# Normalised tokens of twelve tiles turned by VectorE and through DRAM, instead of by TensorE, between two attention loops

## The chip, the cores and the metric

The kernel runs on one core of a Trainium2 chip. The engines that matter here are TensorE (PE in the profile, with its weight loads as PEld), VectorE (DVE), ScalarE (ACT), GpSimd (POOL) and SyncE (SP), which issues nearly all transfers. Each engine works its instructions off in the order in which the built program has them; where one needs another's result it waits at that place, and all that stands behind it on its engine waits with it. The metric is the device time of one execution, in microseconds.

## The reference

Four layers with residuals act on x, 2048 tokens by 576 features: A, B, A, B. A is multi-query attention with 32 query heads of 18 and one shared key and value head; B is a linear attention with a learned feature map. Both begin with a layer norm without weights:

```python
def _layernorm(x, axis=-1, eps=1e-5):
    m = jnp.mean(x, axis=axis, keepdims=True)
    v = jnp.var(x, axis=axis, keepdims=True)
    return (x - m) / jnp.sqrt(v + eps)
...
def _A_ref(x, wq, wk, wv, wo):
    q = (x @ wq).reshape(B, S, H, Dh).transpose(0, 2, 1, 3)
    k = x @ wk
    v = x @ wv
    p = softmax(einsum("bhqd,bkd->bhqk", q, k) * (Dh ** -0.5))
    o = einsum("bhqk,bkd->bhqd", p, v)
    return o.transpose(0, 2, 1, 3).reshape(B, S, H * Dh) @ wo
...
x = x + _A_ref(_layernorm(x), A_wq, A_wk, A_wv, A_wo)
x = x + _B_ref(_layernorm(x), B_wqkv, B_w_phi, B_wo)
x = x + _A_ref(_layernorm(x), A_wq, A_wk, A_wv, A_wo)
x = x + _B_ref(_layernorm(x), B_wqkv, B_w_phi, B_wo)
```

The case concerns the step from the first B to the second A: the layer norm of the second A, and the products with `wq`, `wk` and `wv` that follow it.

## The kernel before

The tokens are cut into 16 tiles of 128. A pair of layers A, B is worked as one **loop** (`attend`), which computes scores, exponentials and sums of attention and, among them, the keys and features of the B layer that follows. There are two such loops, up to about 1217 us and from about 1450 us on. The stretch **between the loops** finishes the first B and prepares the second A, and only it is changed. (Behind the second loop the same read-out runs without the preparation.)

Between the loops each token tile is a job, `token_tile(i)`, a Python generator that gives up its turn at each `yield STAGE`:

- It loads the tile's features from DRAM (`load_features`, L698 and L699, `pht`) and its residual (`xt`).
- `read_out` multiplies features by the state (L804), divides by the denominators (L811 to L813) and copies the last 64 columns a second time (L814). The result `xo` is turned by five TensorE transposes into PSUM (`transposed`, L307 four at once, L311 the last), and split into an upper and a lower half, `xs`, by ScalarE (L132, L313) and VectorE (L135, L316). The output projection follows (L257, 28 matmuls), and VectorE adds it to the residual (L321).
- `next_queries`: `ln_stats` on VectorE (L283 to L286), POOL's power for the reciprocal root (L288), the bias `lnb` on VectorE (L290); `layer_norm` on ScalarE writes `xn` (L297) and copies its last 64 columns a second time (L298). `xn` is in the pool `bw`, with one buffer. Five TensorE transposes turn it, and the two halves go to `xsc`, 9 slots by 256 tokens, which two tiles share.
- After every second tile `project_queries` is queued: 5 blocks of 14 matmuls (L452), whose results ScalarE copies out (L474) and VectorE splits and squares (L478, L479), transfers to the query store `qd` (L481) and to the keys (L486), then values and norms (L492 to L503), stored to `mxd` (L504). The text calls the block of tiles 2p and 2p+1 query block p.

The rows of one block are the 14 products of an upper or lower slot with an upper or lower weight; the third of them is the first that reads a lower slot of the tokens:

```python
PRODUCTS = [p for k in range(4) for p in ((k, 0, k), (k, 1, k), (5 + k, 0, k))]
PRODUCTS += [(4, 0, 4), (4, 1, 4)]
```

`pipelined` starts one job a round and lets each active job do one stage a round, then the queued late work (query blocks). So a round with a query block is long and the next one is short; a pair of them handles two tiles. A scheduling pass then orders the instructions of each engine by dependencies, buffers and estimated durations. Between the loops nothing else fixes that order, except TensorE's in `leave`, at its beginning.

The second way of turning a tile, used inside the loops, exists already: `block_transpose` turns 32x32 blocks on VectorE (L702) and writes the blocks to their places in the DRAM tile `flipped` with four transfers (L707); `fetch_tokens` reads them back with the features on the partitions, in three transfers (L720, L722).

After the last query block `first_queries` loads the queries and shifts of the first chunk of the second loop, `q0` (in the room of `wclo`) and `q1` (in that of `xs`), by L558 and L565.

Of the kernel before, what the change touches and what calls it, by code (L numbers as in the profile page):

```python
# [9 lines left out]
F32 = mybir.dt.float32  # L10
# [3 lines left out]
AF = mybir.ActivationFunctionType  # L14
# [5 lines left out]
P = 128  # L20
S = 2048
D = 576
H = 32
DH = 18
NT = S // P
KT = 5
# [26 lines left out]
STAGE = None  # L53
# [9 lines left out]
def kernel(ctx, tc, x_in, wq, wk, wv, wo, wqkv, w_phi, wob, out):  # L63
    nc = tc.nc
    V, A, T, G = nc.vector, nc.scalar, nc.tensor, nc.gpsimd
# [6 lines left out]
    bw = ctx.enter_context(tc.tile_pool(name="bw", bufs=1))  # L72
# [57 lines left out]
    def split(dst_hi, dst_lo, src, hi_engine, lo_engine):  # L130
        if hi_engine is A:
            A.activation(dst_hi, src, AF.Copy)  # L132
        else:
            hi_engine.tensor_copy(dst_hi, src)
        lo_engine.tensor_sub(dst_lo, src, dst_hi.bitcast(F32))  # L135
# [137 lines left out]
    def run(gen):  # L273
        for _ in gen:
            pass

    def ln_stats(tiles):
        n = len(tiles)
        mv = small.tile([P, n, 2], F32, name=f"mv{n}", bufs=5)
        for j, i in enumerate(tiles):  # L280
            bn = small.tile([P, 2, 6], F32, name="bnst")
            for s in range(2):
                V.bn_stats(bn[:, s, :], xres[i][:, s * HALF : (s + 1) * HALF])  # L283
            V.bn_aggr(mv[:, j, :], bn)
        var = small.tile([P, n], F32, name=f"var{n}", bufs=5)
        V.tensor_scalar(var, mv[:, :, 1], EPS, None, op0=ALU.add)  # L286
        rstd = small.tile([P, n], F32, name=f"rstd{n}", bufs=5)
        G.tensor_tensor(rstd, var, neghalf[:, :n], op=ALU.pow)  # L288
        bias = small.tile([P, n], F32, name=f"lnb{n}", bufs=5)
        V.scalar_tensor_tensor(bias, mv[:, :, 0], -1.0, rstd, op0=ALU.mult, op1=ALU.mult)  # L290
        return {i: (rstd[:, j : j + 1], bias[:, j : j + 1]) for j, i in enumerate(tiles)}

    def layer_norm(i, stats, pool, E, tag="xn"):
        rstd, bias = stats[i]
        xn = pool.tile([P, 5 * P], F32, name=tag)
        if E is A:
            A.activation(xn[:, :D], xres[i], AF.Identity, scale=rstd, bias=bias)  # L297
            A.activation(xn[:, D:], xn[:, 512:D], AF.Copy)  # L298
        else:
            V.tensor_scalar(xn[:, :D], xres[i], rstd, bias, op0=ALU.mult, op1=ALU.add)  # L300
            V.tensor_copy(xn[:, D:], xn[:, 512:D])
        return xn

    def transposed(xn, xs, ps, hi_engine, lo_engine=V):
        pa = ps.tile([P, 4, P], F32, name="ps")
        for k in range(4):
            T.transpose(pa[:, k, :], xn[:, k * P : (k + 1) * P], idf)  # L307
        split(xs[:, 0:4, :], xs[:, 5:9, :], pa, hi_engine, lo_engine)
        yield -440
        pb = ps.tile([P, P], F32, name="ps")  # L310
        T.transpose(pb, xn[:, 512:], idf)  # L311
        if hi_engine is A:
            A.activation(xs[:, 4, :], pb, AF.Copy)  # L313
        else:
            V.tensor_copy(xs[:, 4, :], pb)
        lo_engine.tensor_sub(xs[64:P, 4, :], pb[64:P, :], xs[64:P, 4, :].bitcast(F32))  # L316
        yield -110
# [6 lines left out]
    flipped = dram.tile([NT, D, P], F32, name="flipped")  # L324
# [115 lines left out]
    def project_queries(p, layer, w, xsc, bw, pool, ps, norms):  # L440
# [15 lines left out]
        if opening:  # L456
# [3 lines left out]
            for n in range(len(PRODUCTS)):  # L460
                if n == TURN:
                    st["turn"]()
# [238 lines left out]
    def block_transpose(blocks, src, dst, pause=0):  # L701
        V.transpose(blocks, src)  # L702
        for _ in range(pause):
            yield
        for q in range(P // 32):
            rows = slice(q * 32, (q + 1) * 32)
            nc.sync.dma_start(dst[:, rows].rearrange("(b f) t -> f b t", f=32),  # L707
                              blocks[rows, :].rearrange("f (b t) -> f b t", t=32))
            yield
# [4 lines left out]
        blocks = bw.tile([P, NKG, P], F32, name="pht").rearrange("p a b -> p (a b)")  # L714
        run(block_transpose(blocks[:, :D], xres[i], flipped[i]))

    def fetch_tokens(i):
        xt = bw.tile([P, KT * P], F32, name="xn").rearrange("p (a b) -> p a b", b=P)
        src = flipped[i]
        nc.sync.dma_start(xt[:, 0:4, :], src[:512].rearrange("(k p) t -> p k t", p=P))  # L720
        for half in range(2):
            nc.sync.dma_start(xt[half * 64 : half * 64 + 64, 4, :], src[512:])  # L722
        return xt
# [98 lines left out]

    def next_queries(i, stats, layer, st, xpool, sp, ps):
        p, tt = divmod(i, PAIR)
        xn = layer_norm(i, stats or ln_stats([i]), xpool, A)
        yield STAGE
        if tt == 0:
            st["xsc"] = sp.tile([P, 9, PW], F32R, name="xsc")
        xsc = st["xsc"]
        yield from transposed(xn, xsc[:, :, tt * P : (tt + 1) * P], ps, A)  # L830
        yield STAGE
        if tt == PAIR - 1:
            st["late"].append(project_queries(p, layer, st["wq"], xsc, bw, sp, ps, st["norms"]))
# [34 lines left out]
            load_shifts(q, layer, 0, g)  # L868

    PREP = 1  # L870
    TURN = 11
    WE = V
    LOE = V
# [330 lines left out]
    with first, tc.tile_pool(name="ps0", bufs=7, space=PSUM) as ps:  # L1204
        sp = s0
        stats = {}

        def first_tile(i):
            if i % PAIR == 0:
                stats.update(ln_stats(range(i, i + PAIR)))  # L1210
            yield from next_queries(i, stats, 0, st, sp, sp, ps)
# [12 lines left out]
        ps = Banks([(ps, "ps")])  # L1224
# [54 lines left out]
    for layer in range(LAYERS):  # L1279
        last = layer == LAYERS - 1  # L1280
        st.update(start_state(bw), added=set(), loaded=set())
        with tc.tile_pool(name="a1o", bufs=2) as a1o:
# [12 lines left out]
            def stream(v, layer=layer):  # L1295
# [71 lines left out]
                def flip(i, stats):  # L1367
                    nonlocal fetched
                    unflipped.remove(i)
                    spoiled.add(i)  # L1370
                    flip_tokens(i, stats)
                    fetched = i, fetch_tokens(i)
# [68 lines left out]
            ps = psx.enter_context(tc.tile_pool(name=f"ps{layer}", bufs=7, space=PSUM))  # L1441
            ps = Banks([(ps, "ps")])
# [6 lines left out]
            with tc.tile_pool(name=f"tail{layer}", bufs=1) as tail:  # L1449
                on = st["heads_in"]()  # L1450
                load_part(on.bitcast(F32), c, 0)
                xn = layer_norm(c - 1, ln_stats([c - 1]), bw, A)
                kept = st["kept"]
                first_keys = keys_in(KEPT, kept, feature_room("featk"), st, ps)
                closing = last_group(st["last"], on, c, ps, tail)
                advance(first_keys)
                next(closing)
                advance(first_keys)
                run(closing)
                advance(first_keys)  # L1460
                xs = bw.tile([P, 9, P], F32R, name="xs2")
                advance(transposed(xn, xs, ps, A, LOE), 2)
                advance(first_keys)
                second_keys = keys_in(c - 1, xs, feature_room("featx"), st, ps)
                advance(second_keys, 2)
                advance(first_keys)
                for b in range(2):
                    po = ps.tile([P, HALF], F32, name="ps")
                    run(project(po, st["wo"], b * HALF, on))
                    add_residual(c, b, po)  # L1470
                stats = ln_stats([c])
                advance(second_keys, 2)

        with psx, tc.tile_pool(name=f"s{layer + 1}", bufs=2) as sp:
            if not last:
                reload_w4(sp)

            def leave():
                xn = layer_norm(c, stats, sp, A, "xo")
                advance(second_keys)  # L1480
                xl = sp.tile([P, 9, P], F32R, name="xs3")
# [42 lines left out]
            def token_tile(i):  # L1524
                pht = room(i)
                load_features(pht, spills[layer], i)
                if i not in left:
                    xres[i] = sp.tile([P, D], F32, name="xt", bufs=6)
                    nc.sync.dma_start(xres[i], xd[i])
                yield STAGE  # L1530
                yield STAGE
                yield from read_out(i, pht, st, sp, ps)
                if last:
                    nc.sync.dma_start(out[i * P : (i + 1) * P, :], xres[i])
                else:
                    nc.sync.dma_start(xd[i], xres[i])
                    yield STAGE
                    yield from next_queries(i, None, layer + 1, st, bw, sp, ps)
# [38 lines left out]
```

## Time and profile before

| | |
|---|---|
| Time, median of 3 | 2676.86 us (2673.14 to 2677.76) |
| Profiled execution | 2676.42 us, span 2674.6 us |
| Mean granted TensorE clock | 0.991 |
| The token tiles between the loops | about 1270 to 1447 us of the span |
| First score of the second loop | 1448.62 us |

All rows come from one execution. A row of the engines' events has the start in us, the duration, the engine (SPq is SyncE's issuing of transfers, its duration that of the issue and not of the transfer), the line, the operation, output<-inputs, shapes and the count; in square brackets the idle time ahead of it and who ended it. The first number of a window's row is its start and end.

### The profile page before, as it was taken

Reading aid. Unit: us, or ns where it says so; the run is one execution under the profiler, and the core shown is the slowest. Engines: PE = TensorE matmul, PEld = TensorE weight load, DVE = VectorE, ACT = ScalarE, POOL = GpSimd, SP = SyncE. Lnnn points to the kernel's source line nnn. Section 1 sums busy time; section 2 is a strip of 40 time slices with the busy share of each in tenths; the row PEclk is TensorE's granted clock in tenths of the full one; section 3 lists DMA queues with packets and bytes.
Section 4 is the critical chain, followed back from the end, with each engine's and each line's share of the span. In section 5 each row is a group of like instructions: output and inputs, shape, how many; then the busy total and the mean of one; then the engine's idle time right before and its main releaser. Section 6 shows DMA issues by size and latency. Waiting matters only on the chain. (4 is left out here: it accounts for less than half of the span.)

```text
span 2674.6 us, 55524 instructions
## 1 busy us (share of the span) xinstructions
PE 2602.2 (97%) x22002; PEld 1442.2 (54%) x22002; DVE 1265.0 (47%) x2871; ACT 2153.8 (81%) x2529; POOL 66.0 (2%) x106
## 2 busy tenths in 40 slices
PE   7989999999999999999999999999999999999999
PEld 6633454445444444438996344444444444444498
DVE  8435354444444444436774424444444444444265
ACT  4588889989999999994334999999999999999821
POOL 1000000000000000002000000000000000000010
PEclk9999999999999999999999999999999999999999
DMA  5466243222222222225643312222222222222164
GB/s 182 144 146 171 70 127 100 59 53 60 60 59 57 55 57 57 59 66 158 188 152 105 105 51 59 60 60 60 59 60 59 60 60 57 56 55 55 48 196 140
DMA packets 491634, 232.97 MB, mean 87 GB/s; under 512 B 237734, under 2 KB 458214, under 8 KB 491366
## 3 DMA queue, kind: packets, MB, share of 16 engines
q1 hardware_dynamic: 489894, 226.37, 31.4%
q8 instruction: 177, 2.90, 0.5%
q10 hardware_dynamic: 1472, 2.95, 0.4%
q14 instruction: 91, 0.75, 0.1%
HBM read 130.62 MB, written 96.67 MB: 85 GB/s over the span
## 5 line engine op out<-in xcount | busy, mean ns | idle before, releaser
L1047 ACT ACTIVATE pt<-sc 128x1024 f32<-128x1024 f32 x2036 | 1923.4, 1054 | 180.4 <-PE sc L574 160.3
L574 PE MATMUL sc<-qst,kst 56*128 56x512 f32 x3840 | 698.6, 452 | 21.0 <-ACT pt L1047 20.6
L574 PEld LDWEIGHTS sc<-qst,kst 56*128 56x128 f32 x3840 | 319.4, 185 | 561.7 <-ACT pt L1047 511.8
L853 PE MATMUL acc<-pt,vst 128*32 128x512 f32 x4096 | 499.8, 600 | 0.1
L853 PE MATMUL ps<-pt,vst 128*32 128x512 f32 x4048 | 486.7, 604 | 6.1 <-DVE featq L607 3.2
L853 PEld LDWEIGHTS ps<-pt,vst 128*32 128x32 f32 x4048 | 109.8, 110 | 234.0 <-issue 226.1
L853 PEld LDWEIGHTS acc<-pt,vst 128*32 128x32 f32 x4096 | 104.6, 109 | 211.7 <-issue 209.2
L321 DVE TENSOR_TENSOR xc<-xc,acc 128x288 f32<-128x288 f32 x60 | 27.3, 455 | 349.5 <-PE acc L257 349.5
L257 PE MATMUL ps<-wahi,xs 128*128 128x288 f32 x702 | 152.5, 304 | 2.5 <-ACT xs L132 1.9
L257 PE MATMUL ps<-wchi,xs 128*128 128x288 f32 x576 | 127.2, 307 | 0.0
L257 PE MATMUL acc<-wdhi,on 128*128 128x288 f32 x540 | 120.6, 309 | 3.3 <-DMA on<-od 3.3
L257 PEld LDWEIGHTS ps<-wahi,xs 128*128 128x128 f32 x702 | 116.1, 190 | 7.1 <-ACT xs L132 2.6
L257 PE MATMUL ps<-walo,xs 128*128 128x288 f32 x390 | 114.9, 297 | 0.0
L452 PE MATMUL ps<-xsc,wbhi 128*128 128x256 f32 x576 | 107.3, 285 | 0.6 <-ACT xsc L132 0.6
L474 ACT ACTIVATE pc<-ps 128x256 fp32r<-128x256 f32 x80 | 30.4, 384 | 94.0 <-PE ps L452 92.5
L257 PEld LDWEIGHTS ps<-wchi,xs 128*128 128x128 f32 x576 | 94.1, 188 | 19.0 <-issue 18.1
L607 DVE COPY featk<-acc 128x288 f32<-128x288 f32 x50 | 22.8, 457 | 172.0 <-PE acc L257 172.0
L132 ACT ACTIVATE xs<-ps 128x512 fp32r<-128x512 f32 x36 | 21.4, 595 | 102.6 <-PE ps L307 102.6
L257 PEld LDWEIGHTS acc<-wdhi,on 128*128 128x128 f32 x540 | 88.8, 189 | 25.0 <-issue 23.6
L257 PE MATMUL acc<-wahi,xs 128*128 128x288 f32 x450 | 100.0, 308 | 0.5
L257 PE MATMUL ps<-wclo,xs 128*128 128x288 f32 x320 | 94.3, 295 | 0.0
L452 PEld LDWEIGHTS ps<-xsc,wbhi 128*128 128x128 f32 x576 | 91.2, 192 | 1.6 <-ACT xsc L132 1.1
(261 smaller groups left out, 3062.3 us busy)
## 6 DMA issues: line engine op xcount, KB each, us to landing
qst<-qd SPq DMA_DIRECT2D x360, 72.0 KB
od<-parts SPq DMA_DIRECT2D x512, 36.0 KB
pht<-phi SPq DMA_DIRECT2D x32, 540.0 KB
qd<-pc SPq DMA_DIRECT2D x64, 256.0 KB
on<-od SPq DMA_DIRECT2D x60, 256.0 KB
phi<-pht SPq DMA_DIRECT2D x104, 144.0 KB
xd<-xc SPq DMA_DIRECT2D x33, 288.0 KB
flipped<-pht SPq DMA_DIRECT2D x112, 72.0 KB
```

The costliest lines, as they stand in the source:

```text
L132: A.activation(dst_hi, src, AF.Copy)
L257: T.matmul(dst, xs[:, slot, :], w[half][:, k, c0 : c0 + HALF], start=(n == 0), stop=(n == last))
L321: V.tensor_add(xr, xr, po)
L452: T.matmul(po, lhs, xsc[:, slot, :], start=(n == 0), stop=(n == LASTP))
L474: A.activation(pc[:, 0, :], po, AF.Copy)
L574: T.matmul(sc, kst[head_rows(h), t * P : (t + 1) * P], q[head_rows(h), h // 2, :], start=True, stop=True)
L607: V.tensor_copy(e[:, hs, 0, :], src)
L853: T.matmul(acc[32 * j : 32 * j + 32, :], vst[:, t, :], pts[j], start=first, stop=last)
L1047: A.activation(pt, sc, AF.Exp, scale=SCALE)
```

## The change

For layer 1, that is between the loops, and for tiles 0 to 11 (`NEAR` is 12), `next_queries` turns `xn` in the second way. ScalarE leaves out the second copy of 64 columns. VectorE turns 32x32 blocks of `xn` into `xb`; four transfers write them to `flipped[i]`; `fetch_tokens` reads them into `xf`, three transfers. `xb` and `xf` are new tiles with one buffer each. One stage later ScalarE and VectorE split `xf` into `xsc`; the sources are in SBUF and no longer in PSUM. Tiles 12 to 15 are handled as before. So sixty TensorE transposes go, and 12 VectorE transposes and 84 transfers come; a tile has one stage more.

```diff
-    def layer_norm(i, stats, pool, E, tag="xn"):
+    def layer_norm(i, stats, pool, E, tag="xn", twice=True):
...
             A.activation(xn[:, :D], xres[i], AF.Identity, scale=rstd, bias=bias)
-            A.activation(xn[:, D:], xn[:, 512:D], AF.Copy)
+            if twice:
+                A.activation(xn[:, D:], xn[:, 512:D], AF.Copy)
...
-    def fetch_tokens(i):
-        xt = bw.tile([P, KT * P], F32, name="xn").rearrange("p (a b) -> p a b", b=P)
+    def fetch_tokens(i, pool=bw, tag="xn", **kw):
+        xt = pool.tile([P, KT * P], F32, name=tag, **kw).rearrange("p (a b) -> p a b", b=P)
...
     def next_queries(i, stats, layer, st, xpool, sp, ps):
         p, tt = divmod(i, PAIR)
-        xn = layer_norm(i, stats or ln_stats([i]), xpool, A)
+        far = layer > 0 and i < NEAR
+        xn = layer_norm(i, stats or ln_stats([i]), xpool, A, twice=not far)
         yield STAGE
+        if far:
+            blocks = sp.tile([P, D], F32, name="xb", bufs=1)
+            run(block_transpose(blocks, xn[:, :D], flipped[i]))
+            xt = fetch_tokens(i, sp, "xf", bufs=1)
+            yield STAGE
         if tt == 0:
             st["xsc"] = sp.tile([P, 9, PW], F32R, name="xsc")
         xsc = st["xsc"]
-        yield from transposed(xn, xsc[:, :, tt * P : (tt + 1) * P], ps, A)
+        part = xsc[:, :, tt * P : (tt + 1) * P]
+        if far:
+            split(part[:, 0:4, :], part[:, 5:9, :], xt[:, 0:4, :], A, V)
+            A.activation(part[:, 4, :], xt[:, 4, :], AF.Copy)
+            V.tensor_sub(part[64:P, 4, :], xt[64:P, 4, :], part[64:P, 4, :].bitcast(F32))
+        else:
+            yield from transposed(xn, part, ps, A)
         yield STAGE
         if tt == PAIR - 1:
             st["late"].append(project_queries(p, layer, st["wq"], xsc, bw, sp, ps, st["norms"]))
...
     PREP = 1
+    NEAR = NT - 4
```

What the scheduling pass makes of it is read from the built programs. The lines of the changed program are one higher than before up to L723, and 14 higher behind `next_queries`. First VectorE ahead of a query block (a round in the middle of the stretch, that of 1346 us in the trace), before:

```order
L321 TENSOR_TENSOR xt<-xt,ps 128x288
L283 BN_STATS bnst<-xt 128x6
L284 BN_AGGR mv_15990<-bnst 128x2
L286 TENSOR_SCALAR var_15995<-mv_15990 128x1
L135 TENSOR_TENSOR xs_15812<-ps,xs_15812 128x512
L316 TENSOR_TENSOR xs_15812<-ps,xs_15812 64x128
L811 TENSOR_SCALAR den<-ps 128x24
L811 TENSOR_SCALAR den<-ps 128x8
L812 RECIPROCAL den<-den 128x24
```

and with the change:

```order
L322 TENSOR_TENSOR xt<-xt,ps 128x288
L283 BN_STATS bnst<-xt 128x6
L135 TENSOR_TENSOR xs_15932<-ps,xs_15932 128x512
L317 TENSOR_TENSOR xs_15932<-ps,xs_15932 64x128
L284 BN_AGGR mv_16111<-bnst 128x2
L286 TENSOR_SCALAR var_16116<-mv_16111 128x1
L290 SCALAR_TENSOR_TENSOR lnb_16120<-mv_16111,rstd_16118 128x1
L703 STREAM_TRANSPOSE xb<-xn 128x576
L135 TENSOR_TENSOR xsc<-xf,xsc 128x4x128
L812 TENSOR_SCALAR den<-ps 128x24
L841 TENSOR_TENSOR xsc<-xf,xsc 64x128
L813 RECIPROCAL den<-den 128x24
```

The bias, the transpose of one tile and the lower half of the tile before it now stand between the statistics and the read-out's division; the bias stood behind the division before, and the lower half of `xsc` in an earlier round.

ScalarE at the same place, before:

```order
L132 ACTIVATE xsc<-ps 128x4x128
L313 ACTIVATE xsc<-ps 128x128
L297 ACTIVATE xn<-xt,lnb_15774,rstd_15772 128x576
L298 ACTIVATE xn<-xn 128x64
L132 ACTIVATE xs_15812<-ps 128x512
L313 ACTIVATE xs_15812<-ps 128x128
L474 ACTIVATE pc<-ps 128x256
```

and with the change:

```order
L132 ACTIVATE xs_15932<-ps 128x512
L314 ACTIVATE xs_15932<-ps 128x128
L297 ACTIVATE xn<-xt,lnb_15765,rstd_15763 128x576
L132 ACTIVATE xsc<-xf 128x4x128
L840 ACTIVATE xsc<-xf 128x128
L475 ACTIVATE pc<-ps 128x256
```

The upper half of `xsc` (L132 from `xf`) has moved behind the layer norm, directly ahead of the copies of the query block that reads it; the layer norm overwrites the `xn` that the transpose L703 above reads. On TensorE the query block (L453) now stands directly behind the read-out (L805) of that same round, where before the five transposes of `xn` stood a round ahead of it.

The last place is SyncE's queue at the end of the stretch, ahead of the second loop, before:

```order
L481 DMA qd_104<-pc 64x2x256
L486 DMA kst<-pc 18x256 x5
L481 DMA qd_104<-pc 128x2x256 x4
L504 DMA mxd_106<-length 32x256
L1070 TENSOR_LOAD safe
```

and with the change:

```order
L505 DMA mxd_106<-length 32x256
L559 DMA wclo_17365<-qd_104 18x8x128 x4
L566 DMA wclo_17365<-mxd_106 2x8x128 x2
L559 DMA xs<-qd_104 18x8x128 x6
L566 DMA xs<-mxd_106 2x8x128 x2
L1084 TENSOR_LOAD safe
```

Four of the six loads of `q0`, its two of shifts and all eight of `q1` have moved behind the store of the last norms.

## The prediction

> **What bounds the kernel now.** I read the page's totals first, then the busy times of the stretch between the loops, then who waits there, then the order of events in one pair of token tiles.
>
> ```profile
> span 2674.6 us, 55524 instructions
> PE 2602.2 (97%) x22002; PEld 1442.2 (54%) x22002; DVE 1265.0 (47%) x2871; ACT 2153.8 (81%) x2529; POOL 66.0 (2%) x106
> ```
>
> The stretch itself, cut in three. After the two times and the length come the busy us (and instructions) of PE, PEld, DVE, ACT and POOL, then PE's granted clock, the DMA share and GB/s:
>
> ```profile
> 1281.40:1338.80 57.40, 57.40 (x653) 55.60 (x652) 41.37 (x131) 22.09 (x56) 3.18 (x6) 1.00 0.63 193
> 1338.80:1361.00 22.20, 22.20 (x244) 21.33 (x242) 16.81 (x56) 7.38 (x18) 1.08 (x2) 1.00 0.55 173
> 1361.00:1446.60 85.60, 85.55 (x852) 82.09 (x851) 61.03 (x187) 29.15 (x72) 3.83 (x7) 1.00 0.42 127
> ```
>
> TensorE is busy without a gap for 165 us at full clock, so it alone sets the pace. VectorE is busy 16.81 of 22.20 us, three quarters. Who waits there (us in total, times, longest):
>
> ```profile
> DVE pc L478 <- ACT pc L474: 22.2, 26, 0.9
> DVE lnb L290 <- POOL rstd L288: 5.6, 14, 0.7
> ACT xsc L132 <- PE ps L307: 16.5, 9, 3.5
> ```
>
> VectorE and ScalarE wait for others, and nobody on TensorE waits for them: before, a tile's split (the two rows `xsc`) is done a round ahead of its product. One pair of rounds on TensorE:
>
> ```profile
> 1338.77 0.60 PE L307 MATMUL ps<-idf,xo 128*128 128x128 f32 x4
> 1341.70 0.66 PE L307 MATMUL ps<-idf,xn 128*128 128x128 f32 x4
> 1346.03 0.60 PE L307 MATMUL ps<-idf,xo 128*128 128x128 f32 x4
> 1346.67 1.48 PE L804 MATMUL ps<-kvb,pht 108*64 108x57 f32 x44
> 1356.68 0.66 PE L307 MATMUL ps<-idf,xn 128*128 128x128 f32 x4
> 1361.01 0.60 PE L307 MATMUL ps<-idf,xo 128*128 128x128 f32 x4
> ```
>
> From 1338.77 to 1361.01 a pair takes 22.24 us: a short round of 7.26 us and a long one of 14.98, which holds the 70 query products between the read-out's end (1348.1) and 1356.6, 8.4 us.
>
> **What TensorE saves.** Sixty transposes go, five of each of twelve tiles. Five take from one group's start to the next:
>
> ```profile
> 1281.44 0.60 PE L307 MATMUL ps<-idf,xn 128*128 128x128 f32 x4
> 1281.99 0.60 PE L307 MATMUL ps<-idf,xo 128*128 128x128 f32 x4
> ```
>
> 0.55 to 0.57 us, so 1.14 a pair and 6.8 in all. One copy of 64 columns a tile goes on ScalarE, which is idle two thirds of the time; it is worth nothing.
>
> **What VectorE gets, and where it stands.** One transpose of 128x576 a tile, priced by the same shape of the second turning routine:
>
> ```profile
> L702 DVE STREAM_TRANSPOSE pht<-xc x28: 778/778/779, 248.3 to 2445.6; 128x576 f32<-128x576 f32 x28
> ```
>
> The work alone would fit: 16.81 + 2×0.78 = 18.4 of 21.1 us. The order does not. In the changed program each round has, on VectorE: residual adds and statistics, `lnb` (which waits for POOL's power), the transpose of tile n, the lower half of the split of tile n−1, and only then the read-out's division and `xo`. ScalarE's layer norm of tile n+1 writes the single `xn` buffer and so waits for that transpose; the upper half of the split stands behind the layer norm, and VectorE's lower half waits for it. The chain is transpose, layer norm, upper half, lower half, with VectorE standing still during the middle two. The durations and the places before:
>
> ```profile
> 1342.56 0.20 DVE L814 COPY xo<-xo 128x64 f32<-128x64 f32 x1
> 1344.83 0.13 DVE L286 TENSOR_SCALAR var<-mv 128x1 f32<-128x1 f32 x1
> 1345.69 0.16 DVE L290 SCALAR_TENSOR_TENSOR lnb<-mv,rstd 128x1 f32<-128x1 f32 x1 [0.24 <-POOL rstd L288]
> 1346.23 0.45 DVE L321 TENSOR_TENSOR xt<-xt,ps 128x288 f32<-128x288 f32 x1
> 1346.72 0.46 DVE L283 BATCH_NORM_STATS2 bnst<-xt 128x6 f32<-128x288 f32 x1
> 1347.62 0.69 DVE L135 TENSOR_TENSOR xs<-ps,xs 128x512 fp32r<-128x512 f32 x1
> 1348.34 0.29 DVE L316 TENSOR_TENSOR xs<-ps,xs 64x128 fp32r<-64x128 f32 x1
> ```
>
> ```profile
> 1345.95 0.87 ACT L297 ACTIVATE xn<-xt,lnb,rstd 128x576 f32<-128x576 f32 x1 [2.79 <-DVE lnb L290]
> 1357.37 0.60 ACT L132 ACTIVATE xsc<-ps 128x512 fp32r<-128x512 f32 x1 [0.32 <-PE ps L307]
> ```
>
> *Short round.* From the variance's end to `lnb`'s end 0.9 to 0.95; transpose 0.80 with its hand-over; layer norm 0.95; upper half 0.68; lower half 0.69; the last slot's part 0.3; statistics and norms moved ahead 0.3. About 4.7 us are put ahead of the `xo` copy, which ended 4.0 us after the round's start (1342.76) and now ends at 8.7. TensorE, without its transposes, wants `xo` at 7.26 − 0.57 = 6.7; the first four transposes don't need that copy, so they start at about 8.3. Delay 1.6 us.
>
> *Long round*, on the same zero. The read-out ends at 10.3 and the products stand right behind it. VectorE, free of the short round at 8.7, has 0.9 of norms, then two adds and two statistics (2.1, till 11.7), the two lower halves of `xs` (1.0, till 12.7), `lnb` (13.65), transpose (14.45), ScalarE's layer norm (15.4) and upper half (16.1), lower half (16.8). The third product reads the lower half, and the first two take 0.22. TensorE idles 6.3 us. With 8.4 of products and 3.7 of output projection the pair ends at 28.8 instead of 22.24: **+6.5**, the saved 1.14 being in it. Query blocks 0 to 4 are so: 5 × 6.5 = +32.5. Here I take the sum of the walked order rather than the busy shares. Its lower bound is the same chain without lag from the short round, worked out as a rival below.
>
> *What is left.* The two remaining far tiles save 1.1. Block 5 waits for tile 11, whose split VectorE has behind tile 15's two adds, two statistics and their sequel: 4 × 0.45 and a little, +1.9, between 0 and 4.2 (the rival's stall).
>
> **The clock.** The nearest idle of TensorE is ahead of this stretch; columns as above:
>
> ```profile
> 1272.00:1273.70 1.70, 0.15 (x3) 0.04 (x1) 1.64 (x7) 0.00 (x0) 0.54 (x1) 1.00 0.75 210
> 1273.70:1277.40 3.70, 3.70 (x17) 3.64 (x18) 1.76 (x5) 1.12 (x2) 2.25 (x3) 0.54 0.42 124
> 1277.40:1281.00 3.60, 3.60 (x60) 3.39 (x60) 2.64 (x9) 0.12 (x1) 0.00 (x0) 1.00 0.50 162
> ```
>
> After 1.55 us of idle the next 3.7 us ran at 0.54, which loses 1.7 us. For five idles of 6 us I take 5 × 1.7 = +8.5; the bounds are none and twice that (two such stretches each), 0 to 17.
>
> [...]
>
> **The way through DRAM.** Seven transfers a tile on SP's queue, 84 in all. The nearest are those of the other turning routine, in a quiet queue: four writes, the read's issue (which waits for the writes) and its last two parts:
>
> ```profile
> 518.28 2.00 SPq L707 DMA_DIRECT2D flipped<-pht  x4
> 521.90 0.38 SPq L720 DMA_DIRECT2D xn<-flipped  x1
> 522.32 1.15 SPq L722 DMA_DIRECT2D xn<-flipped  x2
> L707 SPq DMA_DIRECT2D flipped<-pht x112: 307/498/2071, 249.1 to 2447.9; - x112
> ```
>
> 5.2 us of issue and then a landing, 2.15 (next part): 7.3. From a transpose in the short round (at 4.1) to its split in the long one (15.4) there are 11.3, the other way some 18. So the trip is covered by the round between, and I cost it at nothing. Were the cover gone, what exceeds 11.3 would count once a pair. SP then has 7 issues more a tile, 3.5 us of some 13; feature loads and residual stores stand behind its wait for the writes.
>
> [...]
>
> **The seam to the second loop.** Before, the first chunk's queries and shifts are loaded early; now four of six and both shifts stand behind the last norms' store:
>
> ```profile
> 1308.97 0.33 SPq L558 DMA_DIRECT2D wclo<-qd  x1
> 1338.16 0.35 SPq L565 DMA_DIRECT2D wclo<-mxd  x1
> 1439.35 0.34 SPq L504 DMA_DIRECT2D mxd<-length  x1
> 1441.50 0.42 DVE L478 TENSOR_TENSOR pc<-ps,pc 128x256 fp32r<-128x256 f32 x1 [0.59 <-DMA mxd<-length]
> 1448.62 0.97 PE L574 MATMUL sc<-wclo,kst 56*128 56x512 f32 x6 [1.04 <-DVE top L508]
> 1449.02 0.34 SPq L504 DMA_DIRECT2D mxd<-length  x1
> ```
>
> The last store is issued at 1449.02; 0.34 + 4 × 0.33 + 2 × 0.35 of issues and 2.15 of landing (1439.35 to 1441.50) give 1453.5 for the first score instead of 1448.62: **+4.9**, and it can't be hidden, since every score of the loop follows.
>
> **Sum:** 32.5 − 1.1 + 1.9 + 8.5 + 4.9 = +46.7, on the profiled execution's 2676.42 (span 2674.6 and 1.8 around it; the median shown, 2676.86, is 0.02% off): **2723 us**.
>
> **Rivals.**
> 1. *No lag from the short round*: only the long round's chain counts. From the add at 1346.23: 0.49 + 0.49 + 1.01 + 0.24 to the variance at 1348.46, `lnb` done 1349.48, transpose 1350.26, layer norm 1351.15, upper half 1351.8, lower half 1352.5; against 1348.1 + 0.2 that is 4.2 idle, 3.1 net. 5 × 3.1 − 1.1 + 1.9 + 4.9 = +21.2, with the clock's 8.5 +29.7: 2698 to 2706. For it: VectorE's free quarter may catch up; against: the read-out stands behind the split in each round.
> 2. *The trip is late*: at the slowest write's 2.07 us, 4 × 2.07 + 1.2 + 1.5 + 2.15 = 13.1, and some queueing for 14: 2.7 over the 11.3, 5 × 2.7 = +13.5 on the forecast, 2737, and to 2750 if feature loads queue too. For it: DMA share 0.63 and 84 issues; against: the trip's 7.3.
> 3. *VectorE's slack absorbs everything*, so TensorE only loses its transposes: 2676.4 − 6.8 = 2669.6, faster. It decides only if the split is done before the read-out's end, that is 4.2 us earlier than the order lets it, and if the seam's loads are hidden. The page of before, where TensorE waits for nobody, speaks for it.
> 4. *Slack absorbs, the seam stays*: −6.8 + 4.9, 2674.5, no change.
>
> **Chances.** Forecast 0.60, first rival 0.17, second 0.10, third 0.06, fourth 0.07. A change under 0.2% (5.4 us) can't be told from none. So faster 0.06, same 0.07, slower 0.87. The forecast's own range is 2707 (clock at nothing, some catching up) to 2735; with the slower trip and the missing lag it is **2692 to 2750**.
>
> **What would show it.** Right: between the loops TensorE idles about 6 us ahead of each block's third product, ending on VectorE's or ScalarE's `xsc`, with a granted clock near 0.5 behind it; VectorE's `xsc` waits for ScalarE about 1.6 us each round; `xo` transposes come 1.6 late; the first score waits for loads. Wrong: no idle ahead of the products; splits waiting on `xf`'s DMA (second rival); a pair of under 22 us (third).

## The result and the profile after

The changed kernel took 2717.58 us (median of four runs, 2715.69 to 2719.53), the kernel before 2675.6 (2673.14 to 2677.76): a ratio of 1.0158, 95% interval 1.0142 to 1.0174, or 42 us more. Forecast were 2723 us and 46.7 more. One execution of the kernel before (4450.90 us) and one of an experiment (3130.80 us) were in a much slower state of the chip, and no ratio here uses them.

The page of the changed kernel, its totals and the row of granted clock in 40 slices:

```profile
span 2717.1 us, 55516 instructions
PE 2613.5 (96%) x21942; PEld 1449.8 (53%) x21942; DVE 1276.1 (47%) x2883; ACT 2151.8 (79%) x2517; POOL 66.3 (2%) x106
PEclk9999999999999999999888999999999999999999
```

TensorE has 60 instructions fewer and is busy 11 us longer, with a lower clock in the slices between the loops. So I cut out that stretch alone: from the end of the first loop's last value product to the first score of the second loop. The row of this window in the trace of before, then in that of the change (columns as in the prediction):

```profile
1216.81:1448.62 231.81, 226.86 (x2463) 218.23 (x2463) 169.87 (x507) 77.63 (x183) 25.17 (x34) 0.99 0.54 167
```

```profile
1214.95:1491.65 276.70, 239.96 (x2403) 227.57 (x2404) 181.94 (x525) 75.62 (x171) 25.47 (x34) 0.91 0.59 164
```

The stretch grew by 44.9 us. The first loop ended 1.9 us earlier in that execution, and the second loop took 0.5 less; together that is the 42.5 by which the span grew. TensorE's share of a stretch can be split in three: idle time (length less busy), the part of its busy time that a lower clock adds (busy times one less clock, summed over windows of some 2 us), and the rest, its work at full clock.

| stretch, us | length | idle | added by the clock | work at full clock |
|---|---|---|---|---|
| before | 231.8 | 5.0 | 1.5 | 225.4 |
| the change | 276.7 | 36.8 | 19.0 | 220.9 |
| difference | +44.9 | +31.8 | +17.5 | −4.5 |

The line between the last two columns moves by about 1 us with the width of the windows.

Who ended the idle time, in the waits of TensorE in the changed kernel between 1281 and 1492 us (us in total, times, longest); before there was none of these up to 1446:

```profile
PE ps L453 <- ACT xsc L132: 15.2, 6, 3.8
PE sc L575 <- DMA wclo<-qd: 5.8, 1, 5.8
PE ps L805 <- DMA pht<-phi: 5.8, 3, 3.0
PE ps L308 <- ACT xn L297: 2.9, 1, 2.9
```

The largest is the one forecast: each of the query blocks 0 to 5 waits for the split, though ahead of its first product and not of its third. The chain ahead of block 1, first VectorE, then ScalarE, then TensorE, from their timelines:

```profile
1335.96 0.15 DVE L286 TENSOR_SCALAR var<-mv 128x1 f32<-128x1 f32 x1
1336.84 0.16 DVE L290 SCALAR_TENSOR_TENSOR lnb<-mv,rstd 128x1 f32<-128x1 f32 x1 [0.72 <-POOL rstd L288]
1337.02 0.78 DVE L703 STREAM_TRANSPOSE xb<-xn 128x576 f32<-128x576 f32 x1
1339.33 0.69 DVE L135 TENSOR_TENSOR xsc<-xf,xsc 128x512 fp32r<-128x512 f32 x1 [1.53 <-ACT xsc L132]
```

```profile
1337.91 0.87 ACT L297 ACTIVATE xn<-xt,lnb,rstd 128x576 f32<-128x576 f32 x1 [2.86 <-DVE xb L703]
1338.68 0.61 ACT L132 ACTIVATE xsc<-xf 128x512 fp32r<-128x512 f32 x1
```

```profile
1339.35 3.65 PE L453 MATMUL ps<-xsc,w 128*128 128x256 f32 x14 [3.19 <-ACT xsc L132]
```

Variance, POOL's power, `lnb`, transpose, layer norm, upper half, and only then the first product, at 1339.35: the order of the forecast, link by link, with its durations (the upper half is done at 1339.29, 3.2 us after the variance's end; 3.4 were forecast). What was not foreseen in size is what follows each such gap. The clock of TensorE around the stall of block 0, which lasted 3.62 us:

```profile
1302.00:1305.60 3.60, 0.01 (x2) 0.00 (x0) 1.33 (x4) 1.40 (x3) 0.54 (x1) 0.90 0.92 291
1305.60:1309.30 3.70, 3.66 (x15) 3.44 (x16) 2.70 (x9) 0.18 (x1) 0.00 (x0) 0.50 1.03 275
1309.30:1313.00 3.70, 3.70 (x24) 3.70 (x24) 1.30 (x4) 1.15 (x3) 0.00 (x0) 0.68 0.88 210
1313.00:1320.60 7.60, 7.60 (x63) 7.60 (x62) 3.47 (x9) 1.16 (x3) 0.00 (x0) 1.00 0.52 146
```

Half rate for 3.7 us and in part for 3.7 more: 1.85 + 1.18 = 3.0 us lost, nearly as much as the gap itself, where 1.7 was taken.

The seam, SP's queue and TensorE in the changed kernel:

```profile
1486.29 0.35 SPq L505 DMA_DIRECT2D mxd<-length  x1
1486.70 1.51 SPq L559 DMA_DIRECT2D wclo<-qd  x4
```

```profile
1491.65 1.85 PE L575 MATMUL sc<-wclo,kst 56*128 56x512 f32 x6 [5.80 <-DMA wclo<-qd]
```

From the last norms' store to the first score 5.4 us, where the forecast had 4.5 (and before the score stood 0.4 ahead of the store).

### The profile page after: what moved, and what is told of

Its sections match the earlier page's. It is cut to its first block, busy times and chain, and to the rows that moved or that the text cites. A ratio compares the mean times of both kernels' runs of the same rounds, so it can differ in the third digit from the quotient of the medians.

```text
span 2717.1 us, 55516 instructions
## 1 busy us (share of the span) xinstructions
PE 2613.5 (96%) x21942; PEld 1449.8 (53%) x21942; DVE 1276.1 (47%) x2883; ACT 2151.8 (79%) x2517; POOL 66.3 (2%) x106
## 5 line engine op out<-in xcount | busy, mean ns | idle before, releaser
L132 ACT ACTIVATE xs<-ps 128x512 fp32r<-128x512 f32 x36 | 21.5, 596 | 126.8 <-PE ps L308 126.8
L453 PE MATMUL ps<-xsc,wbhi 128*128 128x256 f32 x576 | 111.7, 292 | 0.7 <-ACT xsc L132 0.7
L608 DVE COPY featk<-acc 128x288 f32<-128x288 f32 x50 | 22.8, 457 | 169.4 <-PE acc L257 169.3
L453 PEld LDWEIGHTS ps<-xsc,wbhi 128*128 128x128 f32 x576 | 95.3, 201 | 1.6 <-ACT xsc L132 1.1
```

The costliest lines, as they stand in the source:

```text
L453: T.matmul(po, lhs, xsc[:, slot, :], start=(n == 0), stop=(n == LASTP))
L608: V.tensor_copy(e[:, hs, 0, :], src)
```

## The experiments

All ratios are against runs of the kernel before on the same chip; the change itself stands at 1.0158.

**One stage more before the query block.**

```diff
         yield STAGE
+        if far:
+            yield STAGE
         if tt == PAIR - 1:
             st["late"].append(project_queries(...))
```

> The change with one stage more for the far tiles between the split and the query block, so that a block's split is done a round ahead of its products. Theory (the products wait because the split stands in their own round, behind VectorE's transpose and ScalarE's layer norm): the idle ahead of query blocks 0 to 4, 3.2 to 3.8 us each in the changed kernel's trace, goes, and with it the half clock behind it, about 3 us each; 5 x 6.5 = 32 at most, less what the late feature loads keep: 2690 us, between 2683 and 2699. Rival (the added work itself, on VectorE, SP's queue or the transfers, is the price): no more than 5 us better than the change, 2712 or more.

Measured: 1.0125 (1.0107 to 1.0142), 2707.07 us where before was 2671.36. The stretch is 267.4 us long, 9.3 less than with the change, not the 28 of the theory. TensorE's waits in this run:

```profile
PE ps L805 <- DMA pht<-phi: 9.8, 3, 5.8
PE ps L308 <- ACT xn L297: 6.9, 1, 6.9
PE sc L575 <- DMA wclo<-mxd: 4.4, 1, 4.4
```

No wait for `xsc` is left: the split's place in the products' own round was the cause of those 15.2 us. But other waits took over, the feature loads above all, and TensorE's idle time in the stretch fell only from 36.8 to 31.0 us. So the theory told where the change's stalls come from, not what is left when they go. Why a feature load is late shows on SP's queue ahead of the longest, which the read-out waited for until 1349.87:

```profile
1333.27 4.72 SPq L487 DMA_DIRECT2D kst<-pc  x6
1338.04 2.06 SPq L482 DMA_DIRECT2D qd<-pc  x4
1340.20 2.72 SPq L708 DMA_DIRECT2D flipped<-xb  x4
1342.96 0.52 SPq L1552 DMA_DIRECT2D xd<-xt  x1
1343.58 0.42 SPq L699 DMA_DIRECT2D pht<-phi  x1
1346.17 0.38 SPq L721 DMA_DIRECT2D xf<-flipped  x1
1346.61 1.14 SPq L723 DMA_DIRECT2D xf<-flipped  x2
1347.79 0.56 SPq L700 DMA_DIRECT2D pht<-phi  x1
```

SP issues almost without a gap. The first half of the load stands behind the key and query stores and the trip's four writes, the second half also behind the trip's reads and their 2 us wait for the writes.

**Filling the gap.** 30 matmuls whose results are overwritten, ahead of each of the blocks 0 to 5:

```diff
                 po = ps.tile([P, PW], F32, name="ps")
+                if layer > 0 and p < NEAR // PAIR and m == KT - 1:
+                    for n in range(30):
+                        T.matmul(po, w[0][:, 0, :P], w[1][:, n % 4, :PW], start=True, stop=True)
```

> The change with 30 idle matmuls (3.6 us at full clock, results overwritten) ahead of each of the query blocks 0 to 5, so that TensorE's clock sees no gap while the split is made. Theory (the stalls cost twice, as idle time and as half clock behind it): the idle stays, filled, the granted clock is 1.0 behind it, and some 3 us a block go, 5 x 3 = 15, less 1 or 2 where the filler outlasts the wait: 2703 us, between 2699 and 2709. Rival (the half clock has another cause, or was no loss, because VectorE sets the pace there anyway): 2717 or slower by the filler.

Measured: 1.0124 (1.0107 to 1.0141), 9 us under the change, though 180 matmuls were added. The stretch is 265.0 us, and what the clock adds fell from 19.0 to 4.3. A window of 3.7 us from block 0's first products on, which was at 0.50 in the change:

```profile
1304.50:1308.20 3.70, 3.48 (x29) 3.41 (x29) 3.08 (x11) 0.77 (x3) 0.00 (x0) 1.00 1.09 268
```

So the half clock came from the gaps, and it was on the path: TensorE set the end. Of its 14.7 us, 11.7 came back. The waits on feature loads also became shorter (4.5 us in all for 8.1 with the change), which this run doesn't explain.

**The seam's loads early.** Priority for the first queries' loads:

```diff
         first_room(st)
-        first_queries(layer, st)
+        with tc.high_priority():
+            first_queries(layer, st)
```

> The change with the first queries' loads for the second loop given priority, so that they stand early on SP's queue again. Theory (the first score waits for them, 5.8 us in the changed kernel's trace against 1.0 for another releaser before): 4.8 less, 2713 us, between 2711 and 2714. Rival (the second loop makes up for a late start, since ScalarE sets its pace): no difference, 2716 to 2719.

Measured: 1.0172 (1.0155 to 1.0189), no faster. The seam itself did go; the first score waited 0.93 us, for `top`. But TensorE's waits elsewhere were:

```profile
PE ps L805 <- DMA pht<-phi: 14.1, 4, 5.5
PE ps L453 <- ACT xsc L132: 9.3, 5, 3.6
```

The first is 5.8 in the change. Twelve loads were issued one after the other (1324.16 to 1328.81), in the midst of the trip's writes, and the feature loads behind them came later. Neither theory was right: the second loop did not make up for a late start, since it took no longer with the loads early (1225.1 us from the first score on, 1225.5 with the change), and the queue took the gain back at least in part. How much stays open: the traced execution is the fastest of the four (2713.40 us; the others 2717.68 to 2719.31), and its stretch is 270.2 us, 6.5 under the change's.

**No turning at all.** The kernel before, with the split reading unturned tokens for the twelve tiles:

```diff
-        yield from transposed(xn, xsc[:, :, tt * P : (tt + 1) * P], ps, A)
+        part = xsc[:, :, tt * P : (tt + 1) * P]
+        if layer > 0 and i < NT - 4:
+            xt = xn.rearrange("p (a b) -> p a b", b=P)
+            split(part[:, 0:4, :], part[:, 5:9, :], xt[:, 0:4, :], A, V)
+            ...
+        else:
+            yield from transposed(xn, part, ps, A)
```

> The kernel before without any turning of the twelve tiles: the split reads the normalised tokens as they lie, so the query products work on unturned tokens; sixty TensorE transposes are left out and nothing is put in their place. It gives what taking them off TensorE can bring. Theory (TensorE sets the pace before, 0.55 us a tile): 6.6 us under the kernel before, 2669 us, between 2667 and 2672. Rival (an order that puts the split into the products' own round costs even without the transpose and the trip): slower than before, 2676 to 2700.

The total, 4102 us, says nothing: with queries made of unturned tokens the program took its other branch at the start of the second loop (TensorE's rows there are of L588, the exact maxima). The stretch stands ahead of that branch:

```profile
1213.07:1440.72 227.65, 221.82 (x2403) 212.93 (x2403) 168.04 (x507) 77.78 (x183) 26.08 (x34) 0.99 0.56 169
```

227.65 against 231.81: 4.2 us less, with 6.4 less work at full clock (221.8 less 2.8 for the clock), and the rest given to a longer wait on one feature load at the start (2.35 for 1.55) and its clock. So some 6.4 us are the ceiling of what taking sixty transposes off TensorE can bring, and an order with a split from SBUF is not slower by itself where, as here, TensorE never waits for `xsc`.

**The work added, nothing taken away.** The kernel before, with VectorE's transpose and the seven transfers of the twelve tiles beside TensorE's transposes, which still feed the split:

```diff
+        if layer > 0 and i < NT - 4:
+            blocks = sp.tile([P, D], F32, name="xb", bufs=1)
+            run(block_transpose(blocks, xn[:, :D], flipped[i]))
+            xf = sp.tile([P, KT * P], F32, name="xf", bufs=1)...
+            nc.sync.dma_start(xf[:, 0:4, :], flipped[i][:512]...)
+            for half in range(2):
+                nc.sync.dma_start(xf[half * 64 : half * 64 + 64, 4, :], flipped[i][512:])
         yield STAGE
```

> The kernel before, with the change's work added and nothing taken away: for the twelve tiles VectorE's transpose, the four writes and the three reads on SP's queue run as well, but the split still takes TensorE's transposes. All first queries' loads stand behind the last norms here too. Theory A (the change's price is the split in the products' own round; the work itself is covered): only the seam, +4.9 on the kernel before, and no wait of TensorE on feature loads. Theory B (SP's queue is the second price: a pair's 14 more issues push the feature loads back, as the changed kernel's two waits of 2.6 and 3.0 us and the 10 us in the run with one stage more show): waits on feature loads of 5 to 12 us in all with half clock behind them, +15 to +30 on the kernel before.

Measured: 1.0070 (1.0051 to 1.0088), 2693.68 us where before was 2675.12. The stretch is 254.6 us, 22.8 longer than before. TensorE's waits between 1281 and 1470:

```profile
PE sc L574 <- DMA xs<-qd: 6.5, 1, 6.5
PE ps L804 <- DMA pht<-phi: 6.2, 3, 3.8
```

The waits on feature loads and the time are theory B's: the trip costs even if nobody reads its result, by the places it takes in SP's queue. The seam's wait both theories had. Seam and feature loads are 12.7 of the 16.7 us by which idle time grew; another 3.1 are waits of TensorE on VectorE's `den` and `mv` and on ScalarE's `xn`. The 22.8 us are about half of what the change loses in the stretch.

**The trip on GpSimd's queue,** alone, with the extra stage, and with a second buffer for `xn` as well:

```diff
-            run(block_transpose(blocks, xn[:, :D], flipped[i]))
-            xt = fetch_tokens(i, sp, "xf", bufs=1)
+            run(block_transpose(blocks, xn[:, :D], flipped[i], queue=nc.gpsimd))
+            xt = fetch_tokens(i, sp, "xf", queue=nc.gpsimd, bufs=1)
```

> The change with the seven transfers a tile issued by GpSimd instead of SP. In its order the split of a block stands a round earlier than in the change, and the first queries' loads are early again. Theory B (SP's queue delays feature loads, the seam's loads and the order made around them): the waits on feature loads and the seam's 4.8 go, and with the earlier split most stalls ahead of the products: 2676 to 2690 where the kernel before has 2676. Theory A (the trip through DRAM is too long by itself, on any queue): 2705 or more.

> As the run before, with one stage more between split and query block. Theory B with both prices gone: TensorE waits nowhere between the loops but for the boundary to tiles 12 to 15 (2.9 us), so between 6.6 under the kernel before and 5 over it: 2670 to 2681 where that has 2676. Theory A: 2700 or more.

> As the run before, with a second buffer for the normalised tokens (odd tiles use a free tile of the feature work), so that the layer norm of tile 12 doesn't wait for the transpose of tile 11. If that wait is the boundary's price, 3 to 7 us less than the run before, and 2668 to 2674 where the kernel before has 2676; if the buffer is not what holds it, no difference between the two.

Measured: 1.0316 (1.0293 to 1.0339), 1.0348 (1.0327 to 1.0368) and 1.0328 (1.0302 to 1.0354), 85 to 93 us over the kernel before. GpSimd in the first of them:

```profile
1360.10 0.69 POOL L708 DMA_DIRECT2D flipped<-xb  x1 [5.11 <-issue]
1363.53 0.67 POOL L708 DMA_DIRECT2D flipped<-xb  x1 [2.74 <-issue]
1368.63 0.67 POOL L708 DMA_DIRECT2D flipped<-xb  x1 [4.43 <-issue]
1369.32 0.57 POOL L288 TENSOR_TENSOR rstd<-var,neghalf 128x1 f32<-128x1 f32 x1
```

From one write's start to the next 3.4 and 5.1 us pass there, and the layer norm's power stands behind the writes: GpSimd stood idle 121.3 us in all ahead of 41 of the 48 writes, and VectorE's `lnb`, the layer norm, the splits and TensorE come after the power (between 1281 and 1535 us TensorE waited 16.5 us for `xsc` and 14.5 for `xo`). The expectations of all three rested on GpSimd being free, which its busy share had suggested. That the feature loads are late because of SP's queue is neither shown nor contradicted by them, since so much else moved. The buffer did what it was for: the wait of tile 12's transposes for `xn`, 17.5 us in the second, is 1.7 in the third, which waits for the split instead (10.7 in one wait).

**Feature loads on ScalarE's queue,** with the extra stage:

```diff
     def load_features(pht, spill, i):
         rows, rest = feature_rows(spill, i)
-        nc.sync.dma_start(pht[: 6 * DH, : NKG - 1, :], rows)
-        nc.sync.dma_start(pht[: 4 * DH, NKG - 1, :], rest)
+        nc.scalar.dma_start(pht[: 6 * DH, : NKG - 1, :], rows)
+        nc.scalar.dma_start(pht[: 4 * DH, NKG - 1, :], rest)
```

> The change with one stage more before the query block (as e1_round) and the feature loads issued by ScalarE's queue instead of SP's. Theory B (feature loads are late because they stand on SP's queue behind the trip's writes and reads): TensorE's waits on feature loads, 9.8 us in e1_round between 1340 and 1400, go, and part of the half clock behind them: 10 to 20 us under e1_round, a ratio to the kernel before of 1.005 to 1.009 where e1_round had 1.0125. Rival C (the loads are late because the transfers themselves are slower beside the trip's small pieces): the waits stay, a ratio of 1.011 or more.

Measured: 1.0119 (1.0098 to 1.0139). TensorE's waits:

```profile
PE ps L308 <- ACT xn L297: 11.2, 1, 11.2
PE ps L453 <- ACT xsc L132: 6.4, 2, 4.2
```

The waits on feature loads are gone (9.8 us to none): it was the queue and not slow transfers, so theory B's mechanism holds and rival C's doesn't. The time hardly moved, so B's forecast of it failed: the normalised tokens of tile 12 and two splits are waited for instead, and the seam's loads still (4.3 us).

**More of the trip on ScalarE's queue.** The feature loads and the four writes there (the first of the two edits below), with the second `xn` buffer; then the reads too (both edits):

```diff
-            run(block_transpose(blocks, xn[:, :D], flipped[i]))
+            run(block_transpose(blocks, xn[:, :D], flipped[i], queue=nc.scalar))
-            xt = fetch_tokens(i, sp, "xf", bufs=1)
+            xt = fetch_tokens(i, sp, "xf", queue=nc.scalar, bufs=1)
```

> As e9_round_feat, with the four writes of the trip on ScalarE's queue too and the second buffer for normalised tokens; the first queries' loads are early again in its order. Theory B: no wait on feature loads, none at the seam, none at tile 12 (6.9 us in e1_round): a ratio of 0.997 to 1.003. Rival C: 1.008 or more. Rival D (ScalarE's splits and layer norms now stand behind issues that wait for VectorE's transposes): TensorE waits on xs and xsc, 1.004 to 1.010.

> As e10_feat_write, with the trip's three reads on ScalarE's queue as well, so that nothing of the change is left on SP's. Theory B: as e10 or a little better, 0.997 to 1.003. Rival D: the reads wait on ScalarE for the writes to land, 2 us a tile with everything behind them, so slower than e10 by 5 us or more.

Measured: 1.0122 (1.0097 to 1.0146) and 1.0171 (1.0154 to 1.0188). In the first no wait on feature loads, tile 12 or the seam's loads is left, and in its place, as rival D had it, but dearer, the read-out's own split:

```profile
PE ps L257 <- ACT xs L132: 9.4, 4, 3.6
PE ps L257 <- DVE xs L135: 8.6, 6, 2.1
```

In the second the first of these is 19.7, and the median is 12 us above the first's, as its rival D had it.

**The rest of the remedies together:** extra stage, feature loads on ScalarE's queue, second `xn` buffer, priority for the seam's loads, trip on SP's queue (the edits above).

> As e9_round_feat (one stage more, feature loads on ScalarE's queue), with the second buffer for normalised tokens and priority for the first queries' loads; the trip stays on SP's queue. In e9 TensorE still waits 11.2 us for the normalised tokens of tile 12, behind the transpose of tile 11 in the single buffer, and 4.3 for the seam's loads. If these are what is left of the price: 15 to 20 us under e9, a ratio of 1.004 to 1.007. If the waits only change their place again: 1.010 or more.

Measured: 1.0180 (1.0163 to 1.0197), slower than most. The twelve early loads stand between the trip's writes again, and a read of `xf` behind them took long to be issued:

```profile
1341.57 5.34 SPq L559 DMA_DIRECT2D wclo<-qd  x6
1346.95 2.44 SPq L559 DMA_DIRECT2D xs<-qd  x6
1349.55 2.22 SPq L708 DMA_DIRECT2D flipped<-xb  x3
1358.25 7.24 SPq L723 DMA_DIRECT2D xf<-flipped  x2
```

One query block then waited 17.5 us for its split, and tile 12's normalised tokens were still waited for, 6.8 us, in spite of the second buffer: the waits changed their place again. Of all versions tried none came to the kernel before; the nearest stands at 1.0119.

## Why the prediction was right, and where its sum was not

Direction, size and place were right: the loss lies between the loops and at the seam, in idle time ahead of the query blocks with half clock behind it. The total agrees to 2 us in the stretch (46.7 forecast, 44.9 measured), but that is partly luck: terms that were too large and terms left out cancel.

| term | forecast | measured | shown by |
|---|---|---|---|
| transposes saved | −6.8 (in the pairs' +6.5 and −1.1) | −4.5; −6.4 without any turning | work at full clock |
| idle ahead of blocks 0 to 4 | 5 × 6.3 | 3.6, 3.2, 3.8, 1.6, 1.6; for the last two some 5.3 if the read-out had been on time (below) | TensorE's timeline |
| late `xo` in the short round | 5 × 1.6 | 0.9 and 0.2, in one pair | the same |
| block 5 | 1.9 | 1.35 | the same |
| half clock | 8.5 (0 to 17) | 17.5 | windows; filling the gap |
| feature loads | 0 | 5.8 (5.5 of it ahead of blocks 3 and 4), with one of 2.3 ahead of it where before had 1.55 | waits; work added alone |
| tile 12 | 0 | 2.9 | waits |
| seam | 4.9 | 5.7 more idle at the first score (5.8 + 0.9 against 1.0) | waits; work added alone |

The forecast's parts of a pair, 6.3 + 1.6 − 1.14, give 6.8, where its walk, with rounded links, gave 6.5.

*The step that failed* is the one on the short round: "About 4.7 us are put ahead of the `xo` copy". The order of a long round was walked twice, for every pair. In the short round ahead of block 1 the transpose stands behind that copy:

```profile
1324.46 0.20 DVE L815 COPY xo<-xo 128x64 f32<-128x64 f32 x1
1324.90 0.76 DVE L703 STREAM_TRANSPOSE xb<-xn 128x576 f32<-128x576 f32 x1
```

Ahead of block 2 it had moved into a time in which VectorE waited anyway (1350.42). So for blocks 0 to 2 VectorE came to the long round without lag, and the stall was that of the first rival: 4.2 by its walk, 3.2 to 3.8 measured, also because TensorE starts on the upper half while the lower one is made (at 1339.35 and 1339.33 in the chain above).

Ahead of blocks 3 and 4 the walked order did come: transpose, layer norm and both halves stand ahead of the copy. For block 3, VectorE and then TensorE:

```profile
1385.86 0.78 DVE L703 STREAM_TRANSPOSE xb<-xn 128x576 f32<-128x576 f32 x1
1391.08 0.17 DVE L815 COPY xo<-xo 128x64 f32<-128x64 f32 x1
```

```profile
1394.27 2.58 PE L805 MATMUL ps<-kvb,pht 108*64 108x57 f32 x44 [2.57 <-DMA pht<-phi]
1398.46 3.65 PE L453 MATMUL ps<-xsc,w 128*128 128x256 f32 x14 [1.61 <-ACT xsc L132]
```

The last `xo` transpose ended at 1391.70. A read-out of 1.48 us right behind it would have ended at 1393.2, and the products began at 1398.46, with the split: an estimated stall of 5.3 us, and by the same working 5.3 for block 4, not far from the 6.3 forecast. Of that time 2.6 and 3.0 us went by in waiting for the feature load and 1.1 and 0.7 in a slower read-out, so that only 1.6 each show as a wait for the split. The step thus held in two pairs of five, and there TensorE's wait for the late `xo` was 1.1 us in one pair and none in the other.

*The clock* came out at 17.5, just above its upper bound of 17; 1.6 of that lies behind the wait for tile 12, which the forecast didn't have. One stretch of half rate a stall was taken from the row at 1273.7; after the stalls of blocks 0 to 2 there was a second, in part. Filling the gaps gave 11.7 us back, which shows the term and that it lies on the path. In the trace of the change the clock was at 0.50 behind the gaps of 3.6, 3.2 and 3.8 us (blocks 0 to 2), at 0.50 behind that of 2.6 us ahead of block 3's read-out and at 0.62 over the 2.2 us behind that of 3.0 us ahead of block 4's, while after 1.35 us ahead of block 5 it stayed at 1.00.

*The trip* was costed at nothing, "covered by the round between". For the trip itself that held in the change: of the seven waits of VectorE's splits of `xf` six ended on ScalarE and one, by the profile, on a residual store, and no wait of a split ended on the transfer. But "feature loads and residual stores stand behind its wait" was left as a remark without a price. In the change TensorE waits 5.8 us on feature loads, but ahead of blocks 3 and 4 the split came later still, so there these waits cost little of their own. Their price shows in the run with the work added alone, where nothing is gained and nothing waits for a split: 6.2 us, beside 6.5 at the seam and 4.8 more added by the clock, of 22.8. The feature loads' waits vanished when their issue alone moved from SP to ScalarE, with the same transfers (9.8 us to none), so SP's time for issuing was the scarce thing here, though the time of the kernel hardly fell (1.0125 to 1.0119).

*The rivals.* The first had the right mechanism for the stall and too little beside it; the second's queueing was there, as a late feature load and not as a split that waits for its transfer. The third and fourth fell with the first wait of a block. The seam was right in place and size, and the place of the loads in the queue made it: with the loads early the wait was gone, and the waits on feature loads had grown from 5.8 to 14.1 us.

*Open:* why the waits on feature loads differ from run to run of like order (5.8, 9.8, 14.1, from one traced execution each), and whether a version with an order written out by hand for VectorE and SP would come under the kernel before. The ceiling for it is 6.4 us, and it wasn't tried.

## What to carry to other kernels

Here work moved off the engine that sets the pace didn't pay with its result made in the round that used it (1.0158), nor with it made a round ahead (1.0125). Read in the built order where each link of the new chain stands, in every round and not in one of each kind, and count the half clock behind each gap on TensorE as well: here some 3 us for each gap of 3 to 4. The trip's transfers cost their places in the issuing queue even when nobody waited for their data (6.2 us of waits on feature loads with the work added alone); list what stands behind such transfers there. Here each remedy only renamed the wait, so little slack was left in the chain, and the ceiling (6.4 us of 2676) says how far it was worth going on.

## What the runs showed of the hardware

- After gaps of 3.2 to 3.8 us (blocks 0 to 2) TensorE ran at 0.50 for 3.7 us and at 0.62 to 0.70 for 3.7 more; after one of 5.8 us in the run with one stage more, at 0.51 for 3.7 and then at 1.00; after the seam's 5.8 us in the change, busy for 3.2 to 3.7 of each 3.7 us, at 0.50 for 11. How long the half rate lasts isn't told by the gap's length.
- A write of 72 KB in pieces of 128 bytes, issued by GpSimd, took it 0.68 us, and ahead of 41 of the 48 it stood idle for 3.0 us on average, for which the trace shows no releaser; on SP's queue the change's four writes of a tile took 1.96 to 3.28 us to issue, 0.5 to 0.8 each. Of GpSimd:

```profile
L708 POOL DMA_DIRECT2D flipped<-xb x48: 665/676/892, 1275.7 to 1492.5; - x48
POOL flipped L708 <- issue: 121.3, 41, 6.7
```
